# Clustered attention and a SoLU layer: the mean of w_out's scaled rows by GpSimd and VectorE in place of fp32 products, with a new order of every queue

## The chip, the cores and the metric

The kernel runs on one core of a Trainium2 chip. The metric is the device time of one execution in microseconds (us). A core has five engines that run side by side, each in the order of its own queue, and that wait for one another through semaphores: TensorE (PE for its products, PEld for its weight loads), VectorE (DVE), ScalarE (ACT), GpSimd (POOL) and SyncE (SP), which here issues nearly all transfers.

## The reference

For 4 batches of 8 heads, 768 tokens and 64 columns a head, each query attends to the keys that have the same nearest centroid (16 a head). The 512 columns of all heads then go through a layer with a normalised SoLU:

```python
q_assign = np.argmax(np.einsum('bhsd,hcd->bhsc', q_n, c_n), axis=-1)
k_assign = np.argmax(np.einsum('bhsd,hcd->bhsc', k_n, c_n), axis=-1)
mask = q_assign[:, :, :, None] == k_assign[:, :, None, :]
scores = np.where(mask, scale * np.matmul(q, k.transpose(0, 1, 3, 2)), -1000000000.0)
attn = softmax(scores)
x = np.matmul(attn, v)      # (3072, 512) after the heads are joined
...
h = x @ w_in                                 # (3072, 1024)
solu = h * softmax(h)
mu, var = mean(solu), mean((solu - mu) ** 2)
ln = (solu - mu) / np.sqrt(var + 1e-06) * g_ln
return ln @ w_out                            # (1024, 512)
```

The kernel doesn't subtract `mu` from every row of `solu`. It scales the rows of w_out by g_ln and subtracts from each of their columns its mean over the 1024 rows, once. That is the same by algebra, and this preparation of w_out is what the change touches.

## The kernel before

**Tiling.** The heads of a batch go in pairs (`b.p`). For each pair the raw q and k are loaded, turned so that the head's columns lie on partitions (`xt`), multiplied with the centroids (`cl`, L457 and L462), and the nearest centroid is made a one-hot row (`tb`, `mx`, `oh`, `ot`). The casts of q and k (`ca`, L443 to L447) and the one-hot rows (`pl`, L518 and L526) are copied into one operand `qk`, so that a product of 80 or 96 rows gives score and mask together. In batch 0 the turning is done by TensorE (`tp`, L394, copied out at L401 as `xa`), later by VectorE (L419). A score bank is 512 columns wide (384 in the first pair): `S` on TensorE (L613), `E` the exponential on ScalarE (L619), then `V`, the product with v (L636), and `N`, the division by the sum on VectorE (L648, L661). There are 294 score banks.

**The layer.** For each of 24 blocks of 128 tokens: the turning of x (`tx`, L691), `h` (L722, four steps a block), the row maximum (`hm`, L728), its exponential (`ex`, L734), `u` (L741), u's turning by a transfer (`tu`, L746), the statistics (`bn`, `ag`, L752 and L756), the factor alpha on POOL (`at`, `al`, L762 to L771), `y` with the prepared w_out (L786), and the scaling of y (`sc`, L801 and L803). These blocks are woven into the attention of the batches behind.

**What sets the order.** The program is written as small named operations. A table, `ORDER`, spells out for each of the five queues which kind of operation comes next (`S2` is two score banks). `AWAY` names those that go to another engine than their default. Nothing is reordered at run time: an engine waits at the head of its queue. SP's transfers go the same way, `ld` (pieces of q and k), `lv` (v), `lo` (w_out, four loads of 512 KB), `li` (w_in, four), with eight transfers under way at most.

**The preparation of w_out.** `g_ln` is turned into a column for each of w_out's eight blocks (`gt`, `gk`). POOL spreads these columns to a width of 32 (`gs`, L579). TensorE multiplies them with w_out's blocks in fp32, in two sets of four (`su0`, `su1`, L585), each block into its own quarter of the partitions. VectorE copies the sums out of PSUM (`sk`, L593), and TensorE multiplies them with a constant matrix (`me`, L596), so that every partition has the mean. Then VectorE makes w_out's eight blocks (`ce`, L599): w_out times g, less the mean. `me` stands in TensorE's queue between score banks, and the first `h` behind it. POOL also makes the bf16 copies of w_in (`wi`, L563), which the first `h` reads.

**The head.** TensorE first runs idle products on zeros: 26 in one piece (`wm`) and 23 fillers one by one (`fl`, both L831).

Of the kernel before, what the change touches and what calls it, by code (L numbers as in the profile page):

```python
# [22 lines left out]
class Weave:  # L23
# [18 lines left out]
    """
    ORDER["PE"] = """
        wm tp fl3 cp fl2 tp2 cl tp fl10 cl fl8 S3 tp2 S2 tp S cq S tp S2 tp2 S2 V3 S cl S tp2 V3 S gt S tp S
        tp S2 cl S2 V2 S V S2 tp S2 tp S2 V2 S V S2 cl S2 V2 S V2 S3 V S2 V2 S2 V S cl S3 su S2 V3 S
        V S3 V3 S2 V S su S2 V S V3 S3 me S3 V4 S3 cl S3 V4 S2 h S h S2 h S h S2 V3 S2 V h S h V S V
        S h S V S V S h S2 V3 S2 V h S2 h V2 S y3 S2 h3 S3 y V3 h V S2 V2 S cl S3 h2 S2 V3 S y2 S V
# [128 lines left out]
def kernel(  # L176
# [1095 lines left out]
```

## Time and profile before

| | us |
|---|---|
| time, median of 3 runs (226.12 to 226.81) | 226.6 |
| span of the profiled execution | 225.3 |
| last product of TensorE ends, about | 222 |
| first score product starts | 9.4 |

The profiled execution's own time isn't recorded apart from its span, from the first instruction to the last. A row of the profile names the line, the engine, the operation and what it writes and reads, then how often, the busy time, the mean of one in ns and the idle time of the engine ahead of it with what ended it. The busy time of TensorE holds products that are still in flight, so a full stretch isn't a stretch without a wait.

```profile
L619 ACT ACTIVATE e<-sps 128x512 bf16<-128x512 f32 (+1 forms) x294 | 150.9, 601 | 14.6 <-PE sps L613 12.1
L585 PE MATMUL hreg<-w_g,w_out_c 128*32 128x512 f32 x16 | 2.5, 605 | 0.0
L593 DVE COPY y<-hreg 128x512 f32<-128x512 f32 x1 | 0.7, 691 | 0.6 <-PE hreg L585 0.6
L579 POOL COPY w_out_c<-g_ln 128x256 f32<-128x256 f32 x1 | 0.4, 391 | 0.0
```

### The profile page before, as it was taken

What the parts mean: (1) busy time and instruction counts of PE and PEld (TensorE: products, weight loads), DVE (VectorE), ACT (ScalarE), POOL (GpSimd) and SP (SyncE); (2) the same over time, 40 slices, a digit from 0 to 9 for tenths busy, and PEclk for the clock granted to TensorE, in tenths of its full rate; (3) what the DMA queues carried; (4) which work ended last, traced back from release to release, by engine and by line L of the source; (5) the groups of instructions that cost most, each with busy time, mean ns of one, the idle gap of its engine ahead of it and who ended that gap; (6) DMA issues with size and microseconds to landing.
All of it is one profiled execution on the core that took longest, in us unless ns stands there. A gap on an engine that the chain in (4) does not pass through costs nothing.

```text
span 225.3 us, 6672 instructions
## 1 busy us (share of the span) xinstructions
PE 217.0 (96%) x2454; PEld 142.4 (63%) x2454; DVE 197.2 (88%) x359; ACT 191.9 (85%) x372; POOL 127.0 (56%) x247
## 2 busy tenths in 40 slices
PE   8999999999899999999999999999999999999994
PEld 7676646676556657666567657676566676755452
DVE  3899888899799998999998999887999889988982
ACT  3779978999969999998989899998899998984363
POOL 3499833684792999654667752855696502123331
PEclk9999999999999999999999999999999999999999
DMA  6998999999899899899999998887970637266923
GB/s 153 316 318 164 243 173 224 312 217 192 141 179 168 195 134 157 161 204 170 193 215 174 148 172 217 178 154 190 235 114 9 83 57 155 70 139 158 180 87 140
DMA packets 125679, 38.80 MB, mean 172 GB/s; under 512 B 115016, under 2 KB 121168, under 8 KB 125648
## 3 DMA queue, kind: packets, MB, share of 16 engines
q1 hardware_dynamic: 123904, 37.87, 83.0%
q10 hardware_dynamic: 1744, 0.52, 1.0%
q8 instruction: 19, 0.31, 0.6%
q14 instruction: 12, 0.10, 0.2%
HBM read 23.11 MB, written 6.29 MB: 130 GB/s over the span
## 4 chain that ended last, share of the span: by engine, by line
PE 73%; DMA 8%; DVE 7%; SPq 4%; ACT 3%; issue 3%; POOL 1%; DVEq 0%; ACTq 0%; POOLq 0%
PE sps L613 21%; PE hreg L722 16%; PE yps L786 15%; PE ops L636 11%; DMA raw<-in_k_dram 4%; PE csc L462 3%; SPq L413 3%; PE hreg L394 2%; ACT e L619 2%; DMA uT<-u 2%; DMA xT<-x 2%; PE idle_p L831 1%; DVE xt L419 1%; DVE u L741 1%; PE hreg L585 1%
## 5 line engine op out<-in xcount | busy, mean ns | idle before, releaser
L619 ACT ACTIVATE e<-sps 128x512 bf16<-128x512 f32 (+1 forms) x294 | 150.9, 601 | 14.6 <-PE sps L613 12.1
L613 PE MATMUL sps<-qk 80*128 80x256 bf16 (+5 forms) x636 | 93.7, 262 | 1.6 <-ACT e L619 0.6
L613 PEld LDWEIGHTS <-qk 80*128 80x128 bf16 (+1 forms) x636 | 51.7, 97 | 32.4 <-issue 9.4
L636 PEld LDWEIGHTS <-e 128*128 128x128 bf16 x1152 | 49.2, 97 | 13.0 <-issue 1.9
L722 PE MATMUL hreg<-w_in_sb,xT 128*128 128x512 bf16 x192 | 53.0, 379 | 1.4 <-DVE u L741 1.3
L636 PE MATMUL ops<-v,e 128*128 128x65 bf16 x1152 | 53.5, 193 | 0.1
L786 PE MATMUL yps<-w_out_c,uT 128*128 128x512 bf16 x184 | 48.7, 379 | 0.6 <-DMA uT<-u 0.4
L741 DVE TENSOR_TENSOR u<-e_sb,hreg 128x1024 bf16<-128x1024 bf16 (+1 forms) x25 | 29.1, 1167 | 4.6 <-ACT e_sb L734 4.5
L526 POOL COPY qk<-oht 32x384 f32<-32x384 f32 (+1 forms) x50 | 24.4, 488 | 15.3 <-DVE oht L506 12.6
L752 DVE BATCH_NORM_STATS2 bs<-u 128x6 f32<-128x512 bf16 x48 | 31.5, 676 | 0.1
L728 DVE TENSOR_REDUCE nmax<-hreg 128x1 f32<-128x1024 f32 x24 | 29.0, 1209 | 2.5 <-PE hreg L722 2.2
L734 ACT ACTIVATE e_sb<-hreg,nmax 128x1024 bf16<-128x1024 f32 x24 | 27.0, 1124 | 4.5 <-DVE nmax L728 4.4
L445 POOL CAST qk<-xt 64x768 bf16<-64x768 f32 (+1 forms) x31 | 25.9, 836 | 4.8 <-DVE xt L401 3.3
L786 PEld LDWEIGHTS <-uT 128*128 128x128 bf16 x200 | 18.1, 97 | 13.0 <-issue 0.7
L419 DVE STREAM_TRANSPOSE xt<-raw 128x768 f32<-128x768 f32 x24 | 22.9, 957 | 3.2 <-POOL v L544 1.5
L768 POOL TENSOR_SCALAR esq<-es,mv 128x1 f32<-128x1 f32 x24 | 8.6, 358 | 29.5 <-DVE mv L756 21.3
L722 PEld LDWEIGHTS <-xT 128*128 128x128 bf16 x192 | 16.5, 97 | 11.9 <-DVE u L741 2.3
L447 POOL TENSOR_SCALAR qk<-xt 64x768 bf16<-64x768 f32 (+1 forms) x28 | 22.9, 819 | 1.7
L661 DVE TENSOR_TENSOR x<-ops,den 128x256 bf16<-128x256 f32 (+1 forms) x39 | 18.9, 485 | 1.3
L762 POOL TENSOR_SCALAR es<-esum 128x1 f32<-128x1 f32 x24 | 5.3, 223 | 26.1 <-ACT e_sb L734 25.6
L544 POOL CAST v<-vf 128x384 bf16<-128x384 f32 x27 | 13.6, 518 | 2.9 <-DMA vf<-in_v_dram 2.3
L771 POOL TENSOR_TENSOR alpha<-esq,halves 128x1 f32<-128x1 f32 x24 | 13.5, 563 | 2.0
(80 smaller groups left out, 170.0 us busy)
## 6 DMA issues: line engine op xcount, KB each, us to landing
vf<-in_v_dram SPq DMA_DIRECT2D x16, 384.0 KB, 4.6
out_dram<-y SPq DMA_DIRECT2D x23, 256.0 KB, 2.4
raw<-in_q_dram SPq DMA_DIRECT2D x50, 96.0 KB, 3.7
raw<-in_k_dram SPq DMA_DIRECT2D x50, 96.0 KB, 3.5
w_g<-in_moe_w_out_dram SPq DMA_DIRECT2D x4, 512.0 KB, 6.2
w_st<-in_moe_w_in_dram SPq DMA_DIRECT2D x4, 512.0 KB, 6.0
raw<-in_q_dram SPq DMA_DIRECT2D x3, 384.0 KB, 6.6
raw<-in_k_dram SPq DMA_DIRECT2D x3, 384.0 KB, 7.3
```

The source lines that it names most:

```text
L419: nc.vector.transpose(xt[:], raws[b, p, i][:].rearrange("p j c -> p (j c)"))
L445: VEC[e].tensor_copy(dst, src)
L526: ins = VEC[e].tensor_copy(dst.bitcast(F32), src.bitcast(F32).unsqueeze(1) .to_broadcast([NB, 2, n // 2]))
L613: nc.tensor.matmul(sps_[n, k][:, c0:c0 + w], side(b, h // 2, 1, h % 2, keys)[r], side(b, h // 2, 0, h % 2, slice(s0 * P, s0 * P + w))[r])
L619: nc.scalar.activation(es[n, k][:, :w], sps_[n, k][:, :w], Act.Exp, scale=exp_scale, bias=-exp_scale)
L636: nc.tensor.matmul(opss[g][:, s, :VW], es[n, k][:, c0:c0 + P], v1[slot(b, h // 2)][:, h % 2, kt, :VW], start=(kt == 0), stop=(kt == n_t - 1))
L722: uses(nc.tensor.matmul(hreg[:, at(f, f2)[1], :], xTs[f][:, dc, :], w_in_sb[:, dc, f2 * FF2:(f2 + 1) * FF2], start=(dc == 0), stop=(dc == ...
L728: uses(nc.vector.tensor_reduce(ff[f, "nmax"][:], pair_of(f), axis=AXY, op=Alu.max, negate=True), *both(f))
L734: uses(nc.scalar.activation(ff[f, "e"][:], pair_of(f), Act.Exp, bias=ff[f, "nmax"][:], accum_out=ff[f, "esum"][:]), *both(f))
L741: uses(nc.vector.tensor_tensor(ff[f, "u"][:, at_], ff[f, "e"][:, at_], pair_of(f)[:, at_], op=Alu.mult), *banks)
L752: nc.vector.bn_stats(ff[f, "bs"][:, f2, :], ff[f, "u"][:, f2, :])
L786: ins = nc.tensor.matmul(dst, ff[f, "uT"][:, at(f, f2)[0] * (n_fc // 2) + c, :], w_out_c[:, fc, cols], start=(fc == chunks[0]), stop=(fc = ...
```

## The change

The scaled rows of w_out are now made in place, once: eight scalings (`gm0` to `gm7`) write w_g times g back to w_g, and seven additions (`ga1` to `ga7`), each on the result of the one ahead, sum the blocks over their 128 rows of partitions. POOL does `gm1`, `gm4`, `gm7` and all additions but `ga2`; VectorE does the other five scalings and `ga2`. The mean's product reads the sum from SBUF, with 1/d_ff in its constant matrix in place of 1/(32 d_ff). `ce` becomes a plain subtraction. `gs`, `su0`, `su1` and `sk` go. The `ORDER` of all five queues and `AWAY` are new. `AWAY` moves ten more casts of q and k, two more of v and one of w_in to VectorE in net, and one scaling of y.

```diff
     ORDER["SP"] = """
-        ld4 lv si ld4 lv lg ld4 lv2 ld4 lo2 ld4 lo ld3 lo ld3 li4 tx ld3 lv3 tx ld4 tu ld9 lv ld tu
...
+        ld4 lv si ld6 lg lv3 ld8 lo4 ld8 li4 tx2 ld7 lv2 tu tx ld6 lv2 tu2 ld10 ou2 tu ld11 tu lv
...
     ORDER["PE"] = """
-        wm tp fl3 cp fl2 tp2 cl tp fl10 cl fl8 S3 tp2 S2 tp S cq S tp S2 tp2 S2 V3 S cl S tp2 V3 S gt S tp S
...
+        fl21 wm fl tp cp tp2 cl tp cl fl cq S2 tp S tp S2 tp S tp S2 tp S tp cl V2 S V S tp S tp S
...
-    def spread_g():
-        nc.gpsimd.tensor_copy(g_cols, g_ln2[:].unsqueeze(2).to_broadcast([P, n_fc, NB]))
-
-    def sum_w_out(r):
-
-        for c in range(4):
-            fc = 4 * r + c
-            uses(nc.tensor.matmul(hreg[c * NB:(c + 1) * NB, 1, :], g_cols[:, fc, :], w_g[:, fc, :],
-                                  start=(r == 0), stop=(r == n_fc // 4 - 1),
-                                  tile_position=(0, c * NB)), 1)
-
-    def keep_sums(e):
-        src = hreg[:, 1, :]
-        wt["sum"] = mo.tile([P, d_model], F32, name="y")
-        uses(nc.scalar.copy(wt["sum"][:], src) if e == "ACT" else
-             nc.vector.tensor_copy(wt["sum"][:], src), 1)
+    def scale_w_out(fc, e):
+        VEC[e].tensor_scalar(w_g[:, fc, :], w_g[:, fc, :], scalar1=g_ln2[:, fc:fc + 1],
+                             scalar2=None, op0=Alu.mult)
+
+    def add_w_out(fc, e):
+
+        if fc == 1:
+            wt["sum"] = mo.tile([P, d_model], F32, name="y")
+        VEC[e].tensor_tensor(wt["sum"][:], w_g[:, 0, :] if fc == 1 else wt["sum"][:],
+                             w_g[:, fc, :], op=Alu.add)
 
     def mean_w_out():
-        uses(nc.tensor.matmul(hreg[:, 2, :], g_mean[:], wt["sum"][:]), 1, 2)
+        uses(nc.tensor.matmul(hreg[:, 2, :], g_mean[:], wt["sum"][:]), 2)
 
     def centre_w_out(fc):
-        uses(nc.vector.scalar_tensor_tensor(out=w_out_c[:, fc, :], in0=w_g[:, fc, :],
-                                            scalar=g_ln2[:, fc:fc + 1], in1=hreg[:, 2, :],
-                                            op0=Alu.mult, op1=Alu.subtract), 2)
+        uses(nc.vector.tensor_tensor(w_out_c[:, fc, :], w_g[:, fc, :], hreg[:, 2, :],
+                                     op=Alu.subtract), 2)
...
-    add("gs", "POOL", 0.35, 20, lambda e: spread_g(), ["gk", "wm"])
-    for r in range(n_fc // 4):
-        add(f"su{r}", "PE", 1.06, 30 + r, (lambda e, r=r: sum_w_out(r)),
-            ["gs", f"lo{2 * r}", f"lo{2 * r + 1}"] + ring_free(1),
-            last_tp[-1:] + [f"su{x}" for x in range(r)])
-    add("sk", "DVE", 0.6, 34, keep_sums, [f"su{n_fc // 4 - 1}"], also={"ACT": 0.48})
-    add("me", "PE", 0.9, 36, lambda e: mean_w_out(), ["sk", "sg"] + ring_free(2), last_tp[-1:])
+    for fc in range(n_fc):
+        add(f"gm{fc}", "POOL", 0.55, 30 + fc, (lambda e, fc=fc: scale_w_out(fc, e)),
+            ["gk", f"lo{fc // 2}"], also={"DVE": 0.4})
+        if fc:
+            add(f"ga{fc}", "POOL", 0.7, 30 + fc, (lambda e, fc=fc: add_w_out(fc, e)),
+                [f"gm{fc}", f"ga{fc - 1}" if fc > 1 else "gm0"], also={"DVE": 0.6})
+    add("me", "PE", 0.9, 36, lambda e: mean_w_out(), [f"ga{n_fc - 1}", "sg"] + ring_free(2), last_tp[-1:])
```

In the rows below the lines of the changed kernel are some 11 higher than before up to the preparation of w_out (L526 becomes L537), and 3 higher behind it. First GpSimd's queue from the end of batch 0's casts to the w_in casts (L563, now L573). In the kernel before, L579 is the spreading of g:

```order
L445 CAST qk_102<-xt 64x6x128
L447 TENSOR_SCALAR qk_102<-xt 64x6x128
L579 COPY w_out_c<-g_ln_115 128x256
L518 COPY qk_102<-w_out_c 16x2x3x64
L447 TENSOR_SCALAR qk_102<-xt 64x6x128
L544 CAST v_3_108<-vf 128x6x64
L445 CAST qk_103<-xt 64x768
L563 CAST w_in_sb<-w_st 128x1024
L447 TENSOR_SCALAR qk_103<-xt 64x768
L526 COPY qk_103<-oht 32x2x192 x2
L563 CAST w_in_sb<-w_st 128x1024 x3
```

In the changed kernel the same place of GpSimd's queue reads, with the scalings at L589 and the additions at L596:

```order
L589 TENSOR_SCALAR w_g<-w_g,g_ln_115 128x512
L529 COPY qk_102<-w_out_c 16x2x3x64
L596 TENSOR_TENSOR y<-w_g 128x512
L456 CAST qk_102<-xt 64x6x128
L529 COPY qk_102<-w_out_c 16x2x3x64
L589 TENSOR_SCALAR w_g<-w_g,g_ln_115 128x512
L596 TENSOR_TENSOR y<-y,w_g 128x512 x2
L589 TENSOR_SCALAR w_g<-w_g,g_ln_115 128x512
L596 TENSOR_TENSOR y<-y,w_g 128x512 x3
L458 TENSOR_SCALAR qk_103<-xt 64x768
L537 COPY qk_103<-oht 32x2x192 x2
L573 CAST w_in_sb<-w_st 128x1024
```

The additions and POOL's three scalings stand between the last one-hot copies of batch 0 (`qk_102`) and the first casts of batch 1 (`qk_103`), and the w_in casts come behind all of them; one of these four is now VectorE's.

On VectorE the place of the first blocks of the layer, around the second product `u` (L741), read before:

```order
L728 TENSOR_REDUCE nmax<-hreg 128x1
L419 STREAM_TRANSPOSE xt<-raw 128x768 x2
L741 TENSOR_TENSOR u<-e_sb,hreg 128x1024
L648 RECIPROCAL den<-ops 128x6
L661 TENSOR_TENSOR x<-ops,den 128x6x64
L752 BN_STATS bs<-u 128x6 x2
L728 TENSOR_REDUCE nmax<-hreg 128x1
```

and reads now, where L731 is the row maximum, L430 the transposition and L744 the product:

```order
L731 TENSOR_REDUCE nmax<-hreg 128x1
L759 BN_AGGR mv<-bs 128x2
L430 STREAM_TRANSPOSE xt<-raw 128x768
L651 RECIPROCAL den<-ops 128x6
L664 TENSOR_TENSOR x<-ops,den 128x6x64
L744 TENSOR_TENSOR u<-e_sb,hreg 128x1024
L430 STREAM_TRANSPOSE xt<-raw 128x768
```

The second of the two transpositions of raw q and k has moved behind `u`, and a normalisation has come ahead of it.

More of the change, by code (lines that the diff above doesn't have):

```diff
@@ L42 @@
+        =pl3.3.0.1 at2 =pl3.3.1.1 pl bl al2 at4 al2 at al2 at al at al2 at al at al
     """
     ORDER["PE"] = """
[L44 to L47 removed]
```

100 lines of the change are left out of this document (56 added, 44 removed).

## The prediction

> **What bounds the kernel now.** I read the totals of the page first, then the chain that ended last, then the busy time by stretch.
>
> ```profile
> span 225.3 us, 6672 instructions
> PE 217.0 (96%) x2454; PEld 142.4 (63%) x2454; DVE 197.2 (88%) x359; ACT 191.9 (85%) x372; POOL 127.0 (56%) x247
> PE 73%; DMA 8%; DVE 7%; SPq 4%; ACT 3%; issue 3%; POOL 1%; DVEq 0%; ACTq 0%; POOLq 0%
> 30.00:40.00 10.00, 9.73 (x127) 5.51 (x124) 8.93 (x18) 7.99 (x16) 2.94 (x4) 1.00 1.03 230
> 60.00:70.00 10.00, 8.68 (x98) 5.43 (x97) 9.92 (x16) 7.72 (x16) 7.53 (x12) 1.00 1.03 154
> 70.00:80.00 10.00, 10.00 (x101) 6.35 (x98) 9.93 (x18) 9.38 (x17) 6.68 (x13) 1.00 1.12 193
> ```
>
> In a stretch's row stand its length, then PE, PEld, DVE, ACT and POOL busy, the granted clock and the DMA's. TensorE is the bound, and nearly everywhere: three quarters of the chain. But three engines are within 15% of each other, so what leaves TensorE is worth its time only where VectorE and ScalarE can follow. The stage that the change touches, 30 to 40 us, is the loosest for ScalarE (7.99) and for GpSimd (2.94).
>
> The times shown have a median of 226.6; the profiled execution spans 225.3. I take the 1.3 between them as what lies around the span, sum in spans, and add it at the end. About 0.3% (0.7 us) is what a measurement of this kernel can tell from no change.
>
> **What the change removes: the products.** In the chain of waits stand the two sets (start, length, what), and in the timeline the loads that the second set met:
>
> ```profile
> 32.27 0.99 PE hreg L585 x8
> 37.31 1.32 PE hreg L585 x8
> 37.58 0.14 PEld L585 LDWEIGHTS hreg<-w_g,w_out_c 128*32 128x32 f32 x4 [0.19 <-DMA w_g<-in_moe_w_out_dram]
> ```
>
> Both sets of fp32 products lie on the chain whole: −2.31. With them go their weights' spreading on POOL and the copy of the sums on DVE (0.69). The mean's two passes stay.
>
> **The w_out loads move behind the k rows of the next batch.** In the timeline:
>
> ```profile
> 29.63 0.98 DVE L419 STREAM_TRANSPOSE xt<-raw 128x768 f32<-128x768 f32 x1 [0.90 <-DMA raw<-in_k_dram]
> 30.66 0.14 PEld L462 LDWEIGHTS csc<-xt,c_bd 128*32 128x32 f32 x4 [0.79 <-DVE xt L419]
> ```
>
> DVE waited 0.90 for the last k rows, which had two 512 KB loads of w_out ahead of them; TensorE then stood 0.79 in front of the cluster products. The new SP order sends all eight pieces of q and k first, and TensorE's order puts these products six score banks later. −0.79, and DVE gets 0.90 back. w_out's last piece landed at 37.6 before (the row above); that last piece now has five pieces of q and k fewer ahead of it in the queue (the first has two more), and its scalings stand at 36 to 38 on the engines: no cost.
>
> **The head.** All but one of the 49 filler products now stand ahead of the first transposes.
>
> ```profile
> 0.97 2.95 PE L831 MATMUL idle_p<-w_out_c 128*128 128x128 bf16 x26 [0.97 <-DVE halves L835]
> 3.85 0.86 PE L394 MATMUL hreg<-ident_f,raw 128*128 128x128 f32 x3
> 4.51 0.36 PE L831 MATMUL idle_p<-w_out_c 128*128 128x128 bf16 x3
> 5.25 1.11 PE L394 MATMUL hreg<-ident_f,raw 128*128 128x128 f32 x6
> 7.17 0.72 PE L831 MATMUL idle_p<-w_out_c 128*128 128x128 bf16 x10
> 9.43 0.79 PE L613 MATMUL sps<-qk 80*128 80x384 bf16 x3 [0.42 <-DVE qk L526]
> ```
>
> The first 26 come every 0.107 ((2.95 − 0.29)/25), those at 7.17 every 0.056 ((0.72 − 0.22)/9), and the three at 4.51 are already near that pace. So 33 of the 48 that now stand ahead take until 4.5, the other 15 another 0.84: the first transposes start at about 5.35 in place of 3.85. Little of it counts, since the second set started only at 5.25 anyway. Behind three transposes at 0.11 and the centroids' at 0.17 it now starts at 5.9: +0.65, which the cluster products, the one-hot rows and the first scores carry on. Between nothing (if the copies ahead of the scores are late anyway) and +1.5; I take +0.65.
>
> **What it adds: eight scalings and seven additions, one behind the other.** The mean's product on TensorE now waits for the last addition, and behind it in TensorE's queue stand the scores, so ScalarE starves too. Six additions and three scalings go to POOL, the rest to DVE. POOL has room at that place:
>
> ```profile
> 27.32 0.98 DVE L419 STREAM_TRANSPOSE xt<-raw 128x768 f32<-128x768 f32 x1 [0.22 <-DMA w_g<-in_moe_w_out_dram]
> 28.22 0.51 DVE L484 TENSOR_REDUCE mx<-cst 128x24 f32<-128x384 f32 x1
> 32.53 0.54 DVE L471 STREAM_TRANSPOSE cst<-csc 128x384 f32<-128x384 f32 x1
> 32.74 0.50 POOL L518 COPY qk<-w_out_c 16x384 f32<-16x384 f32 x1 [3.60 <-DVE w_out_c L503]
> 40.89 1.02 PE L596 MATMUL hreg<-y,g_mean 128*128 128x512 f32 x2
> 41.24 1.04 POOL L563 CAST w_in_sb<-w_st 128x1024 bf16<-128x1024 f32 x1 [5.41 <-DMA w_st<-in_moe_w_in_dram]
> ```
>
> It waited 3.60 and 5.41 there, 9.0 in all. What a wide two-input operation costs on POOL this trace does not show. The cast of 1024 columns with one input takes 1.04, so 512 take 0.52: the lower bound. Two inputs read in turn would double it, 1.04: the upper one. I take 1.04, since the one two-tensor row on POOL, one column wide, is also the dearer of its kind:
>
> ```profile
> L768 POOL TENSOR_SCALAR esq<-es,mv 128x1 f32<-128x1 f32 x24 | 8.6, 358 | 29.5 <-DVE mv L756 21.3
> L771 POOL TENSOR_TENSOR alpha<-esq,halves 128x1 f32<-128x1 f32 x24 | 13.5, 563 | 2.0
> L445 POOL CAST qk<-xt x31: 505/820/1152, 7.0 to 167.0; 64x768 bf16<-64x768 f32 x29, 64x384 bf16<-64x384 f32 x2
> L447 DVE TENSOR_SCALAR qk<-xt 64x768 bf16<-64x768 f32 (+1 forms) x3 | 1.4, 461 | 0.0
> L599 DVE SCALAR_TENSOR_TENSOR w_out_c<-w_g,g_ln,hreg 128x512 bf16<-128x512 f32 x8 | 5.4, 732 | 0.0
> ```
>
> Six of them and three scalings of 0.52 are 7.8 of POOL's 9.0: by amount they fit. By order it is tight. The second addition is DVE's (between 0.46 and 0.73; I take 0.6), and the last five on POOL follow it. On DVE, all that stood ahead of the transposition at 32.53 still stands ahead of it, and beyond that three scalings (0.4 each, between the 0.46 of 768 columns and the 0.73 above), two casts of 0.74, one normalisation of 0.6, one tile copy of 0.54 and two one-hot copies of 0.46, less two v casts of 0.44 and a memset of 0.38: 3.5, less 0.5 because an instruction starts some 0.08 before the one ahead ends (28.22 against 27.32 + 0.98). So it ends at 32.53 + 3.0 − 0.90 + 0.65 + 0.6 = 35.9. Then a hop of 0.1, five additions, one scaling and gaps of 0.05: 35.9 + 0.1 + 5.2 + 0.5 + 0.2 = 41.9. TensorE itself would be there at 40.89 − 2.31 − 0.79 + 0.65 + 0.2 (one more score bank ahead) = 38.6. So the mean's product starts at 41.9, **1.0 later than before, with 0.2 more done: +0.8 in place of −2.5**. The adds, not the products, then set this stage. With 0.52 an addition it would be 39.3: −1.8.
>
> The page "GPSIMD Engine Reference" of the Trainium skill (section 3.1) speaks against the change: a two-input addition pays for both inputs passing one read port, some 2.6 cycles an element, and 4497 ns for 2048 columns. An estimate from that page is 1.12 us for 512; by it the mean starts at 42.3, and the sum below would be 0.4 higher, 227.2, still inside the case that I forecast. Its table in section 1 also has POOL share its SBUF port with VectorE's two-input operations; by the row of L445 above (shortest, median and longest in ns) POOL's casts do stretch at times, so the trace agrees as far as it goes.
>
> **Behind it.** POOL's w_in casts follow the adds. From the adds to the third w_in cast stand one cast of q or k at 0.82, three one-hot copies of 0.5, another cast and three w_in casts of 1.04: ready at 48.4, and DVE's fourth about then.
>
> ```profile
> 31.92 1.57 ACT L619 ACTIVATE e<-sps 128x512 bf16<-128x512 f32 x3 [1.09 <-PE sps L613]
> 46.79 0.60 PE L722 MATMUL hreg<-w_in_sb,xT 128*128 128x512 bf16 x2
> ```
>
> The first w_in product stood at 46.8 behind 70 score banks. It now stands behind 74; an exponential comes every 0.48 ((1.57 − 0.6)/2), so four more make it 48.7. Cost nothing, with no margin: each us that POOL is later is then a us of TensorE.
>
> **Order of the FFN on DVE.** In the trace
>
> ```profile
> 60.01 0.98 DVE L419 STREAM_TRANSPOSE xt<-raw 128x768 f32<-128x768 f32 x1 [1.55 <-POOL v L544]
> 60.92 1.18 DVE L741 TENSOR_TENSOR u<-e_sb,hreg 128x1024 bf16<-128x1024 bf16 x1
> 62.16 1.47 PE L722 MATMUL hreg<-w_in_sb,xT 128*128 128x512 bf16 x6 [1.32 <-DVE u L741]
> ```
>
> a transposition that waited 1.55 held up the product u behind it, and TensorE stood 1.32. The new order puts u first. But DVE arrives later (below), so that u starts near 60.3, not 59.2: −0.6, between 0 and −1.3.
>
> **Work moved from POOL to DVE.** DVE gets 18 instructions more: ten casts (five of q at 0.74, five of k at 0.5: 6.2), five scalings (2.0), one addition 0.6, two v casts 0.9, one w_in cast about 0.9, a scaling of y 0.7, two copies out of PSUM 0.9; it loses the sums' copy 0.7, a memset 0.4, and a blanking and a one-hot copy 0.8. Net +10.3 on 197.2, of which about 6.0 behind the first row maximum.
>
> ```profile
> L445 DVE CAST qk<-xt 64x768 bf16<-64x768 f32 x1 | 0.7, 743 | 0.0
> L544 DVE CAST v<-vf 128x384 bf16<-128x384 f32 x5 | 2.2, 437 | 0.0
> 49.60 1.23 DVE L728 TENSOR_REDUCE nmax<-hreg 128x1 f32<-128x1024 f32 x1
> 150.00:160.00 10.00, 10.00 (x113) 6.65 (x111) 7.63 (x15) 9.04 (x18) 5.01 (x11) 1.00 0.94 186
> 160.00:170.00 10.00, 9.78 (x118) 6.33 (x116) 9.53 (x16) 9.53 (x19) 9.28 (x15) 1.00 0.83 156
> 170.00:180.00 10.00, 10.00 (x122) 6.87 (x119) 8.76 (x15) 9.56 (x20) 5.83 (x13) 1.00 0.36 47
> 180.00:190.00 10.00, 10.00 (x143) 7.24 (x141) 8.90 (x15) 9.37 (x19) 1.33 (x4) 1.00 0.54 89
> ```
>
> About half of the 6.0 fall between 150 and 190, where DVE is idle for 5.2, and 2.3 into the last 20 us. I cost this at nothing. If the cover is gone, DVE sets the pace: with the 4.3 added ahead of its first row maximum, less the waits that go there, it comes to that some 1.6 late, and up to 7.6 would have to be found. POOL in turn loses thirteen casts, and was the loaded one at 160 to 170 (9.28). Centring without the multiplication I take at the same 0.73 (gain 0 to 0.15 each, on DVE).
>
> **The sum.** Removed products, loads, head and the wait for the adds together: +0.8. Product u earlier: −0.6. Moved work: 0. 225.3 + 0.2 = 225.5, and with the 1.3 around it **226.8**: what TensorE saves is given back in front of the mean.
>
> **The rivals.**
>
> *The adds are hidden* (an addition near 0.52, or DVE ahead of my count). The mean starts at 39.3, −1.8, and DVE, earlier too, gives u another −0.2: 225.3 − 1.8 − 0.8 + 1.3 = 224.0. For it: POOL's 9.0 of waits, enough for all of it. Against it: two inputs, and an order that crosses between two engines. It decides below 0.86 an addition: five in a row at 0.18 less are the 0.9 that makes it faster by 0.3%.
>
> *DVE becomes the bound* from the first row maximum to the end, the slower side. Price: of the 7.6 above, what its idle time cannot take. The row of 60 to 70 is for it: DVE at 9.92 and TensorE down to 8.68. The row of 70 to 80 is against it: DVE at 9.93 and TensorE full. If a quarter isn't covered, +1.9: 228.7. It counts as slower from 0.5 uncovered.
>
> *The adds collide with DVE's work on SBUF*, also slower: the longest cast on POOL (1.152) exceeds the median (0.820) by 0.33. If each addition grew so, to 1.37, the mean would start at 43.6, and the w_in casts follow: +1.7, 228.5. It decides above 1.14 an addition (five times 0.10 over the forecast is slower by 0.3%). Against it: a median so near the shortest full cast.
>
> *The order gives nothing by itself*: the stalls of TensorE behind 70 us are already small (the rows above read 9.8 to 10.0), so a new order can hardly win more there than the 1.3 named; I see no case below 223.5.
>
> **How the numbers follow.** My forecast, the adds in front of the mean, has 0.36: 226.8, 225.5 to 227.7 by the bounds of u and of the head. Hidden adds 0.32, 224.0. DVE bound 0.18, 228.7. Collisions 0.10, 228.5. Others 0.04. Faster by over 0.3% (below 225.9): 0.32 and 0.06 of the forecast, 0.38. Within: 0.25 of the forecast and 0.02, 0.27. Slower (above 227.3): 0.05, 0.18, 0.10 and 0.02, 0.35. Cases of both signs hold most of the chance, so the range runs from 223.7 to 228.9, and leaves some 0.2 out at its ends.
>
> **What would show it.** The mean's product (two fp32 passes): its start at 41.9, its wait named as GpSimd's addition, some 3 us, ScalarE idle behind it; at 39.3 without wait the second case holds. The additions' row on POOL: 1.04 or 0.52. The first transposes at 5.35, the first scores at 10.1. No wait of the cluster products for k's transposition near 30. The first w_in product near 48.7. DVE's total near 207.5; TensorE's stretches from 70 on below 9.5 with DVE at 9.9 would mean the third case. A wait for w_out's transfers in front of a scaling would upset the whole count of that stage.

## The result and the profile after

The changed kernel takes 235.38 us (median of 4 runs, 233.49 to 236.42) against 226.7 for the kernel before in the same series: a ratio of 1.038 (95% interval 1.032 to 1.044). The 226.7 is the median of four runs, one of which (229.66) was in a slower state that the ratio leaves out. The changed kernel is slower, and by more than the forecast's range reached. The profiled execution took 235.39 with a span of 233.5, 8.2 longer than before.

From the page of the changed kernel: busy time of the engines, the granted clock of TensorE in 40 slices of 5.8 us (tenths, 9 is 90% or more), and the chain that ended last:

```profile
PE 220.7 (95%) x2438; PEld 146.0 (63%) x2438; DVE 208.9 (89%) x377; ACT 191.8 (82%) x372; POOL 131.7 (56%) x242
...
PEclk9999995759999999999999999999999999999999
...
PE 69%; DVE 12%; POOL 8%; issue 4%; ACT 3%; DMA 3%; SPq 0%; ACTq 0%; POOLq 0%; DVEq 0%
```

TensorE is busy 3.7 us *longer* although products are gone, and its clock is not full at one place. The busy time by stretch shows that it is the changed stage and nothing else (length, then PE, PEld, DVE, ACT and POOL busy, granted clock, DMA):

```profile
30.00:40.00 10.00, 7.65 (x86) 4.97 (x83) 9.69 (x18) 6.87 (x14) 9.18 (x9) 0.81 0.82 180
40.00:50.00 10.00, 7.21 (x48) 4.63 (x47) 6.34 (x11) 5.26 (x11) 9.63 (x10) 0.67 0.40 126
50.00:60.00 10.00, 9.76 (x111) 6.45 (x109) 6.99 (x15) 7.77 (x17) 5.36 (x8) 0.84 0.59 98
...
70.00:80.00 10.00, 9.88 (x127) 6.82 (x126) 9.58 (x15) 9.48 (x20) 6.74 (x14) 1.00 1.04 179
```

GpSimd, at 2.94 of 10 before, is now full from 30 to 50. In the timeline of TensorE (start, length; in brackets the idle time ahead and who ended it):

```profile
36.05 0.55 PE L616 MATMUL sps<-qk 80*128 80x256 bf16 x2 [1.51 <-POOL qk L456]
...
46.87 2.07 PE L600 MATMUL hreg<-y,g_mean 128*128 128x512 f32 x2 [2.49 <-POOL y L596]
...
57.31 0.60 PE L725 MATMUL hreg<-w_in_sb,xT 128*128 128x512 bf16 x2
```

TensorE waits twice, 1.51 at the first scores of pair 3 and 2.49 at the mean's product. That product, at 46.87 instead of 40.89, takes twice its time. The first w_in product comes at 57.31 instead of 46.79: +10.5. From it to the end of the span it is 233.5 − 57.3 = 176.2, against 225.3 − 46.8 = 178.5 before: −2.3. So the whole loss lies ahead of the first w_in product, and I use that point as the mark in all runs.

What the two waits do to the clock shows when the stretch is cut where the recorded clock changes:

```profile
34.50:36.12 1.62, 0.11 (x2) 0.10 (x2) 1.62 (x3) 0.60 (x1) 1.49 (x3) 1.00 0.57 85
36.12:42.95 6.83, 6.23 (x65) 4.91 (x65) 6.65 (x13) 4.30 (x8) 6.64 (x6) 0.50 0.92 317
42.95:46.36 3.41, 1.13 (x10) 0.59 (x7) 2.40 (x5) 2.22 (x5) 3.25 (x3) 1.00 0.41 80
46.36:53.19 6.83, 6.32 (x44) 3.50 (x44) 2.43 (x5) 2.77 (x5) 6.55 (x10) 0.50 0.01 2
```

Each wait goes with 6.83 us at half clock, which begin at its end or within it. And this is what stands in GpSimd's queue from 30.6 on:

```profile
30.63 1.57 POOL L589 TENSOR_SCALAR w_g<-w_g,g_ln 128x512 f32<-128x512 f32 x1
...
33.21 1.37 POOL L596 TENSOR_TENSOR y<-w_g 128x512 f32<-128x512 f32 x1 [0.43 <-DVE w_g L589]
...
36.43 1.60 POOL L589 TENSOR_SCALAR w_g<-w_g,g_ln 128x512 f32<-128x512 f32 x1
38.00 2.67 POOL L596 TENSOR_TENSOR y<-y,w_g 128x512 f32<-128x512 f32 x2
40.66 1.86 POOL L589 TENSOR_SCALAR w_g<-w_g,g_ln 128x512 f32<-128x512 f32 x1
42.49 4.33 POOL L596 TENSOR_TENSOR y<-y,w_g 128x512 f32<-128x512 f32 x3
```

Three scalings are 5.03 and six additions, with the short gaps among them, 8.37, together 13.4 us where the forecast had 7.8, in a gap of 9.0. With a cast and two one-hot copies between them the row ends at 46.82, and the mean's product follows 0.05 later.

### The profile page after: what moved, and what is told of

Its sections match the earlier page's. It is cut to its first block, busy times and chain, and to the rows that moved or that the text cites. A ratio compares the mean times of both kernels' runs of the same rounds, so it can differ in the third digit from the quotient of the medians.

```text
span 233.5 us, 6656 instructions
## 1 busy us (share of the span) xinstructions
PE 220.7 (95%) x2438; PEld 146.0 (63%) x2438; DVE 208.9 (89%) x377; ACT 191.8 (82%) x372; POOL 131.7 (56%) x242
## 4 chain that ended last, share of the span: by engine, by line
PE 69%; DVE 12%; POOL 8%; issue 4%; ACT 3%; DMA 3%; SPq 0%; ACTq 0%; POOLq 0%; DVEq 0%
PE sps L616 20%; PE yps L789 16%; PE hreg L725 14%; PE ops L639 10%; PE csc L473 4%; ACT e L622 2%; POOL y L596 2%; PE idle_p L834 2%; DMA xT<-x 2%; DVE xt L412 1%; POOL w_g L589 1%; DVE cst L482 1%; POOL qk L537 1%; DMA raw<-in_k_dram 1%; DVE u L744 1%
## 5 line engine op out<-in xcount | busy, mean ns | idle before, releaser
L616 PE MATMUL sps<-qk 80*128 80x256 bf16 (+5 forms) x636 | 102.3, 268 | 3.8 <-POOL qk L456 1.5
L639 PEld LDWEIGHTS <-e 128*128 128x128 bf16 x1152 | 53.5, 100 | 12.9 <-DVE x L664 2.5
L639 PE MATMUL ops<-v,e 128*128 128x65 bf16 x1152 | 58.9, 196 | 0.8 <-DVE x L664 0.8
L725 PE MATMUL hreg<-w_in_sb,xT 128*128 128x512 bf16 x192 | 54.7, 379 | 0.4 <-DMA xT<-x 0.4
L789 PE MATMUL yps<-w_out_c,uT 128*128 128x512 bf16 x184 | 49.4, 378 | 0.0
L537 POOL COPY qk<-oht 32x384 f32<-32x384 f32 (+1 forms) x50 | 25.5, 510 | 21.9 <-DVE oht L517 13.4
L744 DVE TENSOR_TENSOR u<-e_sb,hreg 128x1024 bf16<-128x1024 bf16 (+1 forms) x25 | 29.2, 1169 | 3.1 <-ACT e_sb L737 2.7
L731 DVE TENSOR_REDUCE nmax<-hreg 128x1 f32<-128x1024 f32 x24 | 29.1, 1212 | 1.8 <-PE hreg L725 1.5
L430 DVE STREAM_TRANSPOSE xt<-raw 128x768 f32<-128x768 f32 x24 | 22.9, 957 | 0.4 <-DMA raw<-in_k_dram 0.4
L456 POOL CAST qk<-xt 64x768 bf16<-64x768 f32 (+1 forms) x25 | 20.5, 820 | 4.7 <-DVE xt L412 3.6
L555 POOL CAST v<-vf 128x384 bf16<-128x384 f32 x25 | 13.0, 531 | 14.4 <-DMA vf<-in_v_dram 13.9
L458 POOL TENSOR_SCALAR qk<-xt 64x768 bf16<-64x768 f32 x21 | 17.9, 854 | 4.6 <-DVE den L651 2.5
L473 PE MATMUL csc<-xt,c_bd 128*32 128x384 f32 (+1 forms) x112 | 12.2, 491 | 0.5 <-DVE xt L412 0.3
```

The lines of the kernel that those rows point to most:

```text
L430: nc.vector.transpose(xt[:], raws[b, p, i][:].rearrange("p j c -> p (j c)"))
L473: nc.tensor.matmul(csc[c * NB:(c + 1) * NB, :n], c_bd[:, p, :], xts[b, p, i][:, lo + part * n:lo + (part + 1) * n], tile_position=(0, c * NB))
L537: ins = VEC[e].tensor_copy(dst.bitcast(F32), src.bitcast(F32).unsqueeze(1) .to_broadcast([NB, 2, n // 2]))
L616: nc.tensor.matmul(sps_[n, k][:, c0:c0 + w], side(b, h // 2, 1, h % 2, keys)[r], side(b, h // 2, 0, h % 2, slice(s0 * P, s0 * P + w))[r])
L639: nc.tensor.matmul(opss[g][:, s, :VW], es[n, k][:, c0:c0 + P], v1[slot(b, h // 2)][:, h % 2, kt, :VW], start=(kt == 0), stop=(kt == n_t - 1))
L725: uses(nc.tensor.matmul(hreg[:, at(f, f2)[1], :], xTs[f][:, dc, :], w_in_sb[:, dc, f2 * FF2:(f2 + 1) * FF2], start=(dc == 0), stop=(dc == ...
```

## The experiments

Three theories: **(1)** the scalings and additions, by their time on GpSimd and VectorE and what they keep waiting, cost it; **(2)** the fall of TensorE's clock behind the waits is a large part of it; **(3)** the new order, head and queues, costs it whatever the operation. Ratios are to the kernel before, run on the same chip in the same series; its median was between 225.42 and 226.7 in these series, so times of different series are best compared by their ratios. e9 leaves g_ln out of its result.

| run | us | ratio, 95% interval | mean's product | first w_in product | mean clock |
|---|---|---|---|---|---|
| before | 226.7 | | 40.89 | 46.79 | 1.000 |
| changed | 235.38 | 1.038, 1.032 to 1.044 | 46.87 | 57.31 | 0.971 |
| e1 products, new order | 226.72 | 1.002, 0.999 to 1.006 | 41.55 | 48.93 | 1.000 |
| e2 adds, old order | 235.55 | 1.041, 1.035 to 1.047 | 46.71 | 54.92 | 0.971 |
| e3 all on VectorE | 237.30 | 1.050, 1.042 to 1.058 | 48.54 | 59.06 | 0.978 |
| e4 idle products | 232.60 | 1.029, 1.022 to 1.035 | 47.36 | 54.83 | 1.000 |
| e5 casts first | 235.85 | 1.050, 1.043 to 1.057 | 47.86 | 57.00 | 0.978 |
| e6 mean later | 235.78 | 1.041, 1.031 to 1.051 | 53.34 | 54.20 | 0.978 |
| e7 products, old head | 226.47 | 1.006, 1.002 to 1.009 | 40.97 | 48.34 | 1.000 |
| e9 no scalings | 231.35 | 1.024, 1.017 to 1.032 | 42.48 | 53.05 | 0.985 |
| e10 fused on VectorE | 230.82 | 1.023, 1.018 to 1.028 | 42.28 | 51.63 | 0.985 |
| e12 fused, idle products | 230.19 | 1.016, 1.010 to 1.022 | 43.02 | 50.94 | 0.998 |

**e1 and e2: order and operation apart.**

```diff
 # e1: the changed kernel's order, the functions of before
-  ... pl2 =ca0.3.1.0 gm =pl0.3.0.0 ga ca pl gm ga2 gm ga3 =ca1.0.1.0 ...   (POOL)
+  ... pl2 =ca0.3.1.0 gs =pl0.3.0.0 ca pl =ca1.0.1.0 ...
-  ... V2 S V S4 V2 S2 V S V S cl S2 V S V S V2 S3 V2 S2 V2 S4 me ...       (PE)
+  ... V2 S V S4 su V2 S2 V S V S cl S2 V S V S V2 su S3 V2 S2 V2 S4 me ...
 # e2: the order of before, the functions of the changed kernel
-  ... ca2 gs pl ca cv ca wi ...                                            (POOL)
+  ... ca2 =gm1 =ga1 pl ca cv ca =gm4 =ga3 =ga4 =gm7 =ga5 =ga6 =ga7 wi ...
-  ... N xt mx xt N oh ot tb pl2 ca N pl xt mx N sk oh ...                  (DVE)
+  ... N xt mx =gm0 xt N oh ot =gm2 tb pl2 =gm3 ca N =ga2 pl xt =gm5 mx N =gm6 oh ...
```

> The changed kernel's order of engines and transfers, with the sums of w_out's rows made by the fp32 products on TensorE again (eight products ahead of the mean's product, one copy on VectorE, the gain applied with the centring) and no scaling or addition. Theory 1 (the additions on GpSimd and VectorE, and what they keep waiting, cost the time): 225 to 228 us, the granted clock back at 1.00, pair 3's first scores without the 1.51 us wait, the mean's product near 42. Theory 2 (the clock of TensorE falls because of the two waits and doubles the cost): the same. Theory 3 (the new order itself, head and queues, costs the time): 232 to 236 us.

> The order of before, with only the operation changed: the same three scalings and six additions on GpSimd and five scalings and one addition on VectorE as in the changed kernel, put where GpSimd was idle; w_out still arrives at 27.1, 29.0, 33.4 and 37.5. Theory 1: slower than before by most of the change's loss, 231 to 235 us, the mean's product waits for the last addition until about 46. Theory 2: a wait of over 1.5 us at the mean's product is followed by a granted clock of about a half for some 6 us. Theory 3: 226 to 228 us.

e1 measures as before, e2 as the changed kernel. Of e1 the stretch from 30 to 40, and from TensorE's timeline the second set of products, the mean's product and the first w_in product:

```profile
30.00:40.00 10.00, 9.66 (x126) 5.82 (x125) 8.43 (x17) 8.34 (x17) 3.86 (x7) 1.00 0.74 180
```

```profile
36.75 1.07 PE L596 MATMUL hreg<-w_g,w_out_c 128*32 128x512 f32 x8
...
41.55 1.02 PE L607 MATMUL hreg<-y,g_mean 128*128 128x512 f32 x2
...
48.93 0.60 PE L733 MATMUL hreg<-w_in_sb,xT 128*128 128x512 bf16 x2
```

The new order carries the products without a wait and at full clock. It starts the first w_in product 2.1 later than before and is 2.0 faster behind it (225.4 − 48.9 = 176.5). **Theory 3 falls: the operation alone costs the 8 to 9 us, in either order.** In e2, TensorE waits 2.91 at the mean's product, with the clock at 0.50 from 40 to 50.

**e4: the clock by itself.**

```diff
-  ... cl S2 V S V S V2 S3 V2 S2 V2 S4 me ...            (PE)
+  ... cl S fk22 S V S V S V2 S3 V2 S2 V2 S4 fk44 me ...
+    add(f"fk{j}", "PE", ..., lambda e: uses(nc.tensor.matmul(hreg[:, 2, :P], idle_w, idle_w[:, :P]), 2), ...)
```

> The changed kernel with idle products of zeros on TensorE, 22 ahead of pair 3's first scores and 44 ahead of the mean's product (each about 0.06 us, written to the third bank of the MoE region, never read), so that TensorE is not idle in the two long waits. The additions and what waits for them are unchanged. Theory 2 (the two waits pull the granted clock to 0.50 for 6.5 us twice, and that costs as much as the waits): the granted clock stays at 1.00, the mean's product takes 1.02 in place of 2.07 us, 229.5 to 232 us. Theory 1 alone (the time of the waits is the price, the clock follows without cost): 234.5 to 236 us.

TensorE's timeline of e4, the mean's product and the first w_in product:

```profile
47.36 1.13 PE L600 MATMUL hreg<-y,g_mean 128*128 128x512 f32 x2 [1.39 <-POOL y L596]
...
54.83 0.60 PE L725 MATMUL hreg<-w_in_sb,xT 128*128 128x512 bf16 x2
```

The clock stays at 1.00, the span falls from 233.5 to 231.2 and the time by 2.8 (medians; the two intervals overlap a little), somewhat less than theory 2 asked for. From the mean's product to the first w_in product it is 7.47 now, 10.44 in the changed kernel and 7.38 in e1. So of the 8.4 by which the changed kernel's first w_in product is later than e1's, about 3.0 are the half clock (10.44 less 7.47); the other 5.3, the late mean's product (46.87 against 41.55), stay.

**e3: all on VectorE.**

```diff
-  ... N xt =pl0.3.0.1 gm pl =gm3 ca gm N ga tb mx gm N oh gm ot ca N ...               (DVE)
+  ... N xt =pl0.3.0.1 gm2 pl ga gm ca N ga gm tb mx N ga gm oh ga gm ot ga gm ca ga gm N ga ...
```

> The changed kernel with all eight scalings and seven additions on VectorE and none on GpSimd. Theory 1 in its narrow form (GpSimd's 1.6 us scalings and 1.3 us additions, each stretched by VectorE beside it, are the price): scalings near 0.40 and additions near 0.60 us, the mean's product at 41 to 43, 227 to 230 us. If VectorE's total is what binds: 7.4 us of work in place of about 3.6 moves its end by 2 to 4 us, and the mean's product stays near 46; 234 us or more.

The narrow form of theory 1 missed, and the trace shows where. The timeline of e3, first VectorE's, then GpSimd's rows, then TensorE's at the mean's product:

```profile
35.56 0.68 DVE L596 TENSOR_TENSOR y<-y,w_g 128x512 f32<-128x512 f32 x1
36.16 0.48 DVE L589 TENSOR_SCALAR w_g<-w_g,g_ln 128x512 f32<-128x512 f32 x1
...
43.22 1.43 DVE L596 TENSOR_TENSOR y<-y,w_g 128x512 f32<-128x512 f32 x1
...
45.76 2.73 DVE L596 TENSOR_TENSOR y<-y,w_g 128x512 f32<-128x512 f32 x1
```

```profile
41.28 1.52 POOL L537 COPY qk<-oht 32x384 f32<-32x384 f32 x2 [8.43 <-DVE oht L517]
...
45.93 2.01 POOL L573 CAST w_in_sb<-w_st 128x1024 bf16<-128x1024 f32 x2
```

```profile
48.54 2.08 PE L600 MATMUL hreg<-y,g_mean 128*128 128x512 f32 x2 [7.36 <-DVE y L596]
```

While GpSimd stood idle (8.43 until 41.28), an addition took 0.68 and a scaling 0.48. When GpSimd worked beside it, the same addition took 1.43 and, beside two w_in casts, 2.73. And VectorE had no room: from 33 to 48.5 it is without a gap. So the additions are late on either engine, and the two hinder each other.

**e8 and e11: the operations alone**, at the end of the kernel before, behind all its work for GpSimd:

```diff
+ e8:  POOL: scaling x3, addition x7           DVE: addition x6
+ e11: POOL: addition x3, scaling x6           DVE, beside the last three: addition, scaling x6
```

> The kernel before, with 3 scalings of a row and 3 additions on GpSimd behind its last alpha, when VectorE has almost nothing left, and then 4 additions on GpSimd beside 6 additions on VectorE; nothing reads them, and the span grows by some 12 us. If the price was the operation itself: scalings 1.57 and additions 1.26 us with VectorE idle. If it was VectorE beside it: scalings 0.5 to 0.8 and additions 1.04, and 1.3 us and more only in the second part. On VectorE beside GpSimd: 0.68 if they don't hinder each other, 1.3 to 2.7 as in the run with all on VectorE if they do.

> The kernel before, with 3 additions and 6 scalings of a row on GpSimd behind its last alpha; beside the last three scalings VectorE does one addition and 6 scalings. Nothing reads them, and the span grows by some 12 us. If the operation itself is the price: GpSimd's scalings 1.57 with VectorE idle, and about the same beside it. If it is VectorE beside it: 1.0 or less alone, 1.6 to 1.9 beside VectorE, whose scalings then take 0.6 to 1.4 us in place of 0.48.

These two took 238.00 and 238.19 us, with the added work at the end. In e8 VectorE's additions ran beside GpSimd's scalings and hardly beside its additions, so GpSimd's additions beside VectorE were not tried; e11 has the scalings with VectorE idle. Per line: shortest, median and longest in ns; the first two rows are of e8, the others of e11:

```profile
L1246 POOL TENSOR_TENSOR w_g<-w_g x7: 1256/1262/1542, 225.9 to 233.9; 128x512 f32<-128x512 f32 x7
L1246 DVE TENSOR_TENSOR w_g<-w_g x6: 681/692/1064, 221.3 to 225.6; 128x512 f32<-128x512 f32 x6
```

```profile
L1242 POOL TENSOR_SCALAR w_g<-w_g,g_ln x6: 1562/1572/1984, 225.0 to 233.2; 128x512 f32<-128x512 f32 x6
L1242 DVE TENSOR_SCALAR w_g<-w_g,g_ln x6: 473/756/902, 230.8 to 234.2; 128x512 f32<-128x512 f32 x6
```

On GpSimd an addition costs 1.26 alone and a scaling 1.57: the price is mostly the operation itself. Beside VectorE's scalings GpSimd's last two took 1.98, and VectorE's own between 0.47 and 0.90. Beside VectorE's additions in e8 GpSimd's three scalings took 1.58 to 1.98, while four of the six additions kept their 0.68 to 0.69 and two took 1.06. So the two engines stretch each other at times, and not in every overlap.

**e5 and e6: take the waits apart.**

```diff
-  ... =ca0.3.1.0 gm =pl0.3.0.0 ga ca pl gm ga2 ...              (POOL, e5 and e6)
+  ... =ca0.3.1.0 =pl0.3.0.0 ca pl gm ga gm ga2 ...
-  ... S4 me S3 V3 S V S cl S3 V4 S4 V2 S2 h ...                 (PE, e6 alone)
+  ... S4 S3 V3 S V S cl S3 V4 S4 V2 S2 me h ...
-  ... N xt2 ce2 N ce tb ce N ce wi ce mx ce2 hm N u ...         (DVE, e6 alone)
+  ... N xt2 N tb N ce3 wi mx ce5 hm N u ...
```

> The changed kernel with GpSimd's first scaling and first addition (3.0 us together) moved behind pair 3's last cast and placement, so that pair 3's first scores no longer wait for them. If that 1.51 us wait and the half clock after it are a third of the loss: 231 to 233 us. If GpSimd's row of scalings and additions as a whole sets the mean's product (it still ends near 46.8, TensorE only arrives earlier and waits longer): 234 to 237 us, one long wait of 4 to 6 us ahead of the mean's product, the granted clock 1.00 until then and about 0.50 for some 6 us after it.

> As e5, and the mean's product is put 15 banks of scores later on TensorE (with the centrings behind three more normalisations on VectorE), so that TensorE need not wait for the last addition. Scalings and additions are the same. Theory that the loss is TensorE's wait at that place with the clock's fall behind it: 227 to 231 us, the granted clock 1.00, the mean's product still near 47. Theory that the engines' extra work and its contention are the loss wherever the product stands: 234 us or more.

e5's premise was wrong: the wait at pair 3's scores remained. From e5's timeline, VectorE's row, then TensorE's:

```profile
35.33 1.61 DVE L456 CAST qk<-xt 64x768 bf16<-64x768 f32 x1
```

```profile
37.03 0.38 PE L616 MATMUL sps<-qk 80*128 80x256 bf16 x2 [1.73 <-POOL y L596]
```

GpSimd's casts and one-hot rows for this pair were done by 33.4, and an addition of the sum can't release scores. VectorE's cast of the same pair ends at 36.94, 0.09 ahead of the scores; in the changed kernel it ends at 35.95 for scores at 36.05, and in e6 at 37.57 for 37.67. In e3, where GpSimd stood idle there, the scores come at 35.20, 0.11 behind VectorE's cast. So the wait is for **VectorE**, behind two scalings (0.61 and 1.38 in the changed kernel) and with the cast itself stretched: 0.54 in e3, 1.17 in the changed kernel, 1.61 here. The profile had named GpSimd. As the other half of the expectation says, the mean's product stayed late (47.86), and no time was won.

In e6 the mean's product waits for nothing and the first w_in product comes 3.1 earlier than in the changed kernel, but the time is the same. TensorE's timeline of e6, then VectorE's:

```profile
53.34 1.02 PE L600 MATMUL hreg<-y,g_mean 128*128 128x512 f32 x2
...
57.14 0.38 PE L725 MATMUL hreg<-w_in_sb,xT 128*128 128x512 bf16 x1 [1.86 <-DVE w_in_sb L573]
...
60.59 0.61 PE L725 MATMUL hreg<-w_in_sb,xT 128*128 128x512 bf16 x2 [1.14 <-DVE w_out_c L603]
```

```profile
54.40 1.89 DVE L603 TENSOR_TENSOR w_out_c<-w_g,hreg 128x512 bf16<-128x512 f32 x3 [2.62 <-PE hreg L600]
56.20 0.89 DVE L573 CAST w_in_sb<-w_st 128x1024 bf16<-128x1024 f32 x1
```

TensorE's waits moved behind the mark, to VectorE's w_in cast and a centring, and what was won there is lost again (180.1 from the mark to the end of the span, against 176.2). But that cast is late by e6's own order: it stands behind three centrings, which need the mean's product, and VectorE was idle for 2.62 just ahead of them. The wait at pair 3's scores and 6.83 us of half clock are left as well. So e6 meets the time of its second theory without showing its cause; whether a later place of the mean's product with the cast ahead of it would win time is not tried.

**e9: the additions without the scalings.**

```diff
-  ... =ca0.3.1.0 gm =pl0.3.0.0 ga ca pl gm ga2 gm ga3 ...                       (POOL)
+  ... =ca0.3.1.0 =pl0.3.0.0 ga ca pl ga2 ga3 ...
-  ... =pl0.3.0.1 gm pl =gm3 ca gm N ga tb mx gm N oh gm ot ca N ...             (DVE)
+  ... =pl0.3.0.1 pl ca N ga tb mx N oh ot ca N ...
```

> The changed kernel without the eight scalings: w_out is centred unscaled, so g_ln is left out of the result. GpSimd's row ahead of the mean's product loses 1.57 + 1.60 + 1.86 = 5.0 us, VectorE 4.3 us. Theory (GpSimd's own row of scalings and additions sets the mean's product, and everything up to the first w_in product moves with it): the mean's product at 41.5 to 43, additions still 1.26 or more, pair 3's first scores without the 1.51 us wait, granted clock 1.00, 225 to 228 us. Rival (the chain of additions on two engines, with contention, sets it also without scalings): the mean's product at 44 or later, 230 us or more.

TensorE's timeline of e9, and the stretch that the recorded clock marks there:

```profile
42.48 2.08 PE L600 MATMUL hreg<-y,g_mean 128*128 128x512 f32 x2 [2.63 <-POOL y L596]
...
53.05 0.60 PE L725 MATMUL hreg<-w_in_sb,xT 128*128 128x512 bf16 x2
```

```profile
42.23:49.06 6.83, 6.58 (x44) 3.54 (x44) 2.50 (x6) 2.77 (x5) 6.55 (x10) 0.50 0.28 44
```

The mean's product came where the theory put it, and pair 3's wait is gone. The time is 3 to 6 us over the expectation and on the side of the rival, though not by its mechanism. The expectation had left out that TensorE, without products, arrives early: it stood at the product from 39.85, waited 2.63, and ran 6.83 at half clock (10.57 from there to the first w_in product, against 7.38 in e1). Even with the row of GpSimd 5 us shorter, it is slower than before.

**e10 and e12: one pass on VectorE**, `sum = w_g · g + sum`, nothing on GpSimd; e12 with idle products ahead of the two waits.

```diff
+            VEC[e].scalar_tensor_tensor(out=wt["sum"][:], in0=w_g[:, fc, :],
+                                        scalar=g_ln2[:, fc:fc + 1], in1=wt["sum"][:],
+                                        op0=Alu.mult, op1=Alu.add)
-  ... ca N tb mx N sk oh ot ca N ...                                  (DVE, against e1)
+  ... ca N ga2 tb ga mx ga N ga oh ga ot ga2 ca N ...
-  ... V S V2 S3 V2 S2 V2 S4 me ...                                    (PE, e12)
+  ... V S V2 S3 fk22 V2 S2 V2 S4 fk22 me ...
```

> The order of the run with products (e1, 226.72 us), without products: one scaling and seven instructions on VectorE that each scale a row and add it in one pass, the centring as before with the gain, nothing on GpSimd. VectorE gets 0.5 + 7 x 0.7 = 5.4 us for the 0.69 us copy ahead of the mean's product, which has about 2.5 us of idle time from 25 to 42 there; TensorE loses 2.3 us of products. Theory (the time ahead of the mean's product on the engine that adds is what counts): the mean's product 1 to 3 us later than in e1, at 42.5 to 44.5, 225.5 to 228.5 us. Rival (VectorE's total binds, as in the run with all on VectorE): 230 us or more.

> The fused sums on VectorE of the run before (230.82 us), with 22 idle products of zeros on TensorE ahead of the values that waited 1.40 us and 22 ahead of the mean's product. VectorE's work is the same. If most of what that run lost against the products (4.1 us) was the half clock that followed the 1.40 us wait: granted clock 1.00, the mean's product still near 42.3, the first w_in product near 49.7 in place of 51.63, 227.3 to 228.8 us. If it was VectorE's extra time ahead of the centring and the casts: the first w_in product stays near 51.5, 230 us or more.

Rows of TensorE's timeline of e10, then of e12:

```profile
38.46 0.54 PE L640 MATMUL ops<-v,e 128*128 128x65 bf16 x12 [1.40 <-DVE x L665]
...
42.28 2.07 PE L600 MATMUL hreg<-y,g_mean 128*128 128x512 f32 x2 [0.47 <-DVE y L595]
```

```profile
43.02 1.08 PE L600 MATMUL hreg<-y,g_mean 128*128 128x512 f32 x2
...
50.94 0.60 PE L726 MATMUL hreg<-w_in_sb,xT 128*128 128x512 bf16 x2
```

The cheapest form of the sums is still slower than the products. e10's mean's product came a little ahead of the expectation (42.28), but its time is the rival's: the normalisation behind the adds made TensorE wait 1.40, and 6.83 us of half clock followed. e12 kept the clock at 1.00 there and won 0.7 at the first w_in product, not the 1.9 expected; the times of the two are not apart. At full clock e12's first w_in product is still 2.0 later than e1's, so that part is not the clock; that it is VectorE's time is argued and not shown (9.83 of 10 busy from 40 to 50, but 9.60 in e1 too). Another 2.1 of e12's 4.1 us fall behind the mark, where TensorE waits 1.52 for a normalisation at 113.8, and are not explained.

**e7: the head.**

```diff
-  fl21 wm fl tp cp tp2 cl tp cl fl cq S2 ...                (PE)
+  wm tp fl3 cp fl2 tp2 cl tp fl10 cl fl8 cq S2 ...
```

> The new order with the fp32 products (as e1, 226.72 us), and the idle products at the start put as before: 26 and 3 ahead, the rest between the transposes. First transposes at 3.9 in place of about 5.7, first scores 9.4 in place of 10.54. If the head is on the path: 225.2 to 226.2 us, 0.5 to 1.1 under e1. If something later takes its place: 226.4 to 227.0 us.

226.47: the first scores came at 9.95 in place of 10.54, the span is 0.9 shorter than e1's, and the time can't be told apart from e1's. No version here beats the kernel before.

## Why the prediction was wrong, step by step

The forecast was 226.8 and the measurement 235.4. In spans it is 225.5 against 233.5, +8.0: the first w_in product was forecast at 48.7 and came at 57.31, +8.6, and the rest was 225.5 − 48.7 = 176.8 against 176.2. The mechanism came as forecast: the additions, not the products, set this stage, and the mean's product waits for GpSimd's last one. What failed is the size of that term, and what hangs on it. That the wait itself was near the forecast (2.49, some 3 forecast) is luck: TensorE arrived at 44.4 and not at 38.6, held up by a wait and a half clock that the forecast doesn't have.

- **Products gone, −2.31: about right.** In e9, without them, TensorE stood at the mean's product from 39.85, 1.7 ahead of e1, where two sets of 1.06 and 1.07 stand on its way.
- **w_out's loads behind k: right.** No wait of the cluster products near 30 is left, and no scaling waited for a transfer.
- **The head, +0.65: too small.** The first transposes came at 5.76 (forecast 5.35), the first scores at 10.62 (10.1): +1.2. It lies inside the bounds given, and e7 finds hardly a price for it.
- **What it adds: here it failed, in the prices.** An addition on GpSimd was put at 1.04, called the upper bound, from a cast doubled; alone it is 1.26. A scaling was put at 0.52, because a cast with one input takes that per 512 columns; alone it is 1.57, *more* than the addition. A scaling on VectorE was put at 0.4; it is 0.48 with GpSimd idle (e3), and was 0.61 to 1.38 in the changed kernel. The mean's product was 46.87 and not 41.9, +5.0: `ga2` ended 1.84 later than forecast (37.74 against 35.9; VectorE's scalings and cast ahead of it), the five additions behind it took 6.8 in place of 5.2, the scaling among them 1.86 in place of 0.52, and the gaps 0.2 more: 1.84 + 1.6 + 1.34 + 0.2. The idle 9.0 of GpSimd into which "by amount they fit" got 13.4. The cast was the wrong nearest row, since it scales nothing. But the trace of before has, listed by lines, a scaling on GpSimd, of k by a constant, and it would have misled as well, at 0.55 for 512 columns:

```profile
L447 POOL TENSOR_SCALAR qk<-xt 64x768 bf16<-64x768 f32 (+1 forms) x28 | 22.9, 819 | 1.7
```

The scaling of w_out differs from it in its factor (one for each partition), its fp32 result written in place, and 128 partitions in place of 64. Which of these makes it 1.57 no run takes apart. The Trainium skill's page "GPSIMD Engine Reference", section 4.1, calls one-input operations there "roughly line-rate"; by the 1.57 of these runs against VectorE's 0.48 this scaling by a column of factors is not. Its section 3.1, from which 1.12 was estimated for an addition, was nearer to the 1.26 than the value taken.

- **Behind it, "each us that POOL is later is then a us of TensorE": too small in size, and along another path.** 5.0 later at the mean's product became 8.6 at the first w_in product. The step that was missing altogether is the clock: about 3.0 of the 3.6 more, by e4. The w_in casts, by which the forecast let GpSimd's lateness reach TensorE, did not hold it up: between the two products TensorE waits for nothing. Nor has the sum a term for the 1.51 at pair 3's scores; it counted VectorE's scalings only as time ahead of `ga2`, and not as time ahead of the cast that these scores need.
- **u ahead of the transposition, −0.6: right in kind.** No wait of TensorE for u near 62 is left, so the whole 1.32 is gone. With the queues behind it the stretch from the first w_in product on is 2.3 shorter than before, in e1 2.0; in e1 all of that is lost again ahead of it (2.1).
- **VectorE's 10.3 us more: about right.** 208.9 measured, 207.5 forecast. Behind the first w_in product VectorE is busy 164.4 us, 159.4 before, and no cost of it is seen there: the stretch is 176.2, against 178.5.
- **The rivals.** "The adds are hidden" falls. "VectorE becomes the bound" from the first row maximum on falls too. "The adds collide with VectorE's work on SBUF" was the nearest: it foresaw an addition of 1.37, and the six took 1.35 in the mean. But it priced neither the scalings nor the clock, so that 228.5 was far short; and most of the price is there without a collision (e8, e11).

How much of the 8.1 that the changed kernel's span exceeds e1's belongs to GpSimd's prices alone, how much to the collision, is not taken apart: at the prices alone GpSimd's nine operations would be 6 × 1.26 + 3 × 1.57 = 12.3, of 13.2 that they took (13.4 with the gaps). Nor does any run take away the wait at pair 3's scores by itself.

## What to carry to other kernels

Before work moves to an idle engine, ask for a row of the same operation, type and operand kinds on *that* engine; where there is none, the bound from a cheaper operation is not an upper bound, and a short run of the operation alone costs little. Idle time of an engine counts only up to the next thing that waits for it: here the mean's product on TensorE, which waits for the last addition. And where a busy TensorE is the bound, a wait of 1.4 us and more can cost twice, once as the wait and again as half clock behind it.

## What the runs showed of the hardware that was not expected

- **Half clock comes in pieces of 3.41 us, and a wait well under that can start it.** Ahead of TensorE's last products the recorded stretches at 0.50 were 6.83 (changed kernel twice, e9, e10), 3.41 and 6.83 (e5, e6), 10.24 (e3) and 13.65 (e2): one to four times 3.41. The shortest waits ahead of them were 1.40 (e10), 1.51 (changed kernel), 1.62 (e6), 1.73 (e5) and 1.79 (e2); one piece in e6, at 10.6, followed the head's many short waits, none over 0.78 once the products had begun. Length alone doesn't decide it: 1.32 in the kernel before, another 1.40 in e3, 1.59 in e11 and 1.86 in e6 had no such stretch behind them. The page "TensorE: Matmul & The Clock Gate" of the Trainium skill, Part 1, tells of a free-running window of 3413 ns, and the pieces agree; its rule of thumb, no gaps over about 3.4 us, did not protect these runs.
- **GpSimd and VectorE can hinder each other both ways, though not in every overlap.** A VectorE addition of 512 fp32 columns took 0.68 alone and 1.43 and 2.73 beside GpSimd's copies and casts (e3), but 0.68 to 0.69 four times of six beside its scalings (e8); a GpSimd scaling 1.57 alone and 1.98 beside VectorE's scalings (e11).
- **This scaling by a column of factors is dearer on GpSimd than an addition of two rows** (1.57 against 1.26), the other way round from VectorE (0.48 against 0.68).
